# Narrowing float64 weights with a shift, a sign pass and an integer add, in a scan-and-feed-forward kernel on one core

## Chip, cores and metric

The kernel runs on one core of one Trainium2 chip. The metric is the device time in microseconds, the median of several runs. A profile records one execution: every instruction of the engines, every transfer, and the clock that TensorE was granted.

The engines are named as the profile names them: PE is TensorE (PEld its weight loads), DVE is VectorE, ACT is ScalarE, POOL is GpSimd, SP is SyncE, whose queue issues most of the DMAs. Each engine works through its own list of instructions in order and waits on semaphores for the others.

## The reference

Two stages. The first is a chunked state-space scan over 4 batches, 8 heads, 768 positions; the second a feed-forward block of 3072 tokens, 256 to 2048 to 256, with the quick form of GELU.

```python
def _attn_ref(x, a, B, C):
    ...
    for c in range(nc):
        ...
        y_intra = np.einsum('bhij,bhjd->bhid', M, xc)
        y_inter = np.einsum('bhin,bhnd->bhid', Cc, state) * decay_to_i[:, :, :, None]
        y[:, :, sl] = y_intra + y_inter
        ...
        state = decay_full[:, :, None, None] * state + np.sum(Bx, axis=2)
    return y.astype(np.float32)

def _moe_ref(x, w_in, w_out):
    h = x @ w_in
    g = h * (1.0 / (1.0 + np.exp(-1.702 * h)))
    return (g @ w_out).astype(np.float32)
```

The output y of the scan, with its heads side by side, is the x of the feed-forward block. `x`, `a`, `B` and `C` arrive as float32. The two weight matrices `w_in` and `w_out` arrive as float64, and every weight must be made into a float32 on the chip, which has no float64 arithmetic.

## The kernel before

Tokens go in six groups of 512 (g = 0 to 5). For each group the scan gives yT, the transposed input of the feed-forward block. Group 0 then takes the plain way: `hidden(0, f)` (L873) makes the 16 slices of 128 hidden units, each by two fp32 products on PE (each recorded as two passes), followed by a silu on ACT; `project_all(0, ...)` (L975) then multiplies by w_out, for f = 0 to 15, with two products for each f: o[0] for the first 128 output columns (c = 0), o[1] for the second 128 (c = 1). Later groups take a way with fewer products and mixed weights (`first`, `product`, `mix_in`, `mix_w`).

The weights are narrowed while group 0 runs. They come in ten pieces (`PIECES`, L154): 0 to 3 are two hidden slices of w_in each (512 columns), 4 and 5 four slices each (1024 columns), 6 to 9 four slices of w_out each (1024 columns; w_out has the layout partition, c, f, e, so a piece is one stretch of f in each of the two halves c). `fetch` (L163) brings a piece as pairs of 32-bit words. The narrowing takes the words apart: the upper word holds sign, 11 bits of exponent and 20 bits of mantissa, the lower word the rest of the mantissa.

- `fields(i)` (L188): two DVE passes. L192 keeps the exponent bits of the upper word, L195 its mantissa bits with a leading one.
- `clamp(i)` (L198): two ACT passes (L203, L204) that turn the exponent field into a float32 power of two; their bias is a tile, `edge`.
- `rounded(i)` (L206): one DVE pass (L208) that adds the scaled lower word to the mantissa.
- `join(i)` (L215): two DVE passes, L222 puts the sign on the power, L228 multiplies both into w_in or w_out.

Buffers: `bits` four deep, the tiles tagged m and p2 two deep.

The order of every engine is written out by hand: `in_order` (L21) chains the instructions of an engine in the order in which the Python code makes them, so where a call stands decides what it is queued behind. Around the start (L1160 to L1207) the calls are: scores and decays of the first two chunk pairs, `fields(0)`, `ends_first`, `rounded(0)`, `score`, `weigh(0)` (L691), `fetch(1, held=True)` with a memset (L171) that holds back the transfers of pieces 1 to 5, `weigh(1)`, `gain`, `parts_first` (ACT, L730), `clamp(0)`, `keep_first` (DVE, the scan L735 and two copies L740 that give the states S), `finish` (PE: L828 from the decays, L816 from S; then ACT, L845, yT), `join(0)` and so on. Afterwards `at(places, f, ...)` hangs work behind a slice f of `hidden` or ahead of step f of `project_all`: `narrow(i)` (L235, which is `rounded`, the `fields` of the next piece, and `join`) behind slices 1, 2, 4, 6, 9 and 12; for pieces 8 and 9 ahead of projection steps 0, 1 and 5 (L1231 to L1236). Ahead of step 0 also stands `turn(PG)`: four transposes on PE (L597, tp), copies on ACT (L590, BT and CT), then a DVE product (L665, CsT) of the next two chunks.

The framework that builds the program finds for each instruction which earlier instructions wrote or read the same memory, and makes it wait for them by semaphores.

Of the kernel before, what the change touches and what calls it, by code (L numbers as in the profile page):

```python
# [8 lines left out]
FP32 = mybir.dt.float32  # L9
U32 = mybir.dt.uint32  # L10
BF16 = mybir.dt.bfloat16
AF = mybir.ActivationFunctionType
ALU = mybir.AluOpType
AX = mybir.AxisListType

GELU_SCALE = 1.702
P = 128
TG = 512

# [16 lines left out]
def kernel(  # L36
# [31 lines left out]
    nc = tc.nc  # L68
# [7 lines left out]
    DM, DF = moe_w_in.shape[0], moe_w_in.shape[1] // 2  # L76
# [8 lines left out]
    PG = CG // 2  # L85
# [97 lines left out]

    mantissa, power = {}, {}

    def fields(i):  # L188
        hi, cols = bits[i][1], slice(0, PIECES[i][2] * DM)
        mantissa[i] = wide.tile([P, PN], U32, tag="m", name=f"m{i}")[:, cols]  # L190
        power[i] = wide.tile([P, PN], U32, tag="p2", name=f"p2{i}")[:, cols]
        nc.vector.tensor_scalar(out=power[i], in0=hi, scalar1=0x7FF00000, scalar2=None,  # L192
                                op0=ALU.bitwise_and)

        nc.vector.tensor_scalar(out=mantissa[i], in0=hi, scalar1=0x000FFFFF,  # L195
                                scalar2=0x00100000, op0=ALU.bitwise_and, op1=ALU.bitwise_or)

    def clamp(i):  # L198


        e = power[i]
        z = e.bitcast(FP32)
        nc.scalar.activation(z, e, AF.Relu, scale=-8.0, bias=edge[:, 0:1])  # L203
        nc.scalar.activation(e, z, AF.Relu, scale=-1.0, bias=edge[:, 1:2])  # L204

    def rounded(i):  # L206

        nc.vector.scalar_tensor_tensor(out=mantissa[i].bitcast(FP32), in0=bits[i][0],  # L208
                                       scalar=2.0 ** -32, in1=mantissa[i],
                                       op0=ALU.mult, op1=ALU.add)  # L210


    NEXT = {1: (6,), 5: (9,)}
# [1 line left out]
    def join(i, parts=1):  # L215

        name, f, n = PIECES[i]
        n //= parts
        low, m, p2 = bits.pop(i)[1], mantissa.pop(i), power.pop(i)
        for k in range(parts):  # L220
            cols, fs = slice(k * n * DM, (k + 1) * n * DM), slice(f + k * n, f + (k + 1) * n)
            nc.vector.scalar_tensor_tensor(out=p2[:, cols], in0=low[:, cols], scalar=0x80000000,  # L222
                                           in1=p2[:, cols], op0=ALU.bitwise_and, op1=ALU.bitwise_or)
            if name == "in":
                dst, h = w_in[:, fs].rearrange("p f k e -> p (f k e)").unsqueeze(1), 1
            else:
                dst, h = w_out[:, :, fs].rearrange("p c f e -> p c (f e)"), 2
            nc.vector.scalar_tensor_tensor(  # L228
                out=dst, in0=m[:, cols].bitcast(FP32).rearrange("p (h e) -> p h e", h=h),
                scalar=2.0 ** -20, in1=p2[:, cols].bitcast(FP32).rearrange("p (h e) -> p h e", h=h),  # L230
                op0=ALU.mult, op1=ALU.mult)
        for n in NEXT.get(i, ()):
            fetch(n)

    def narrow(i):  # L235
        rounded(i)
        if i + 1 < len(PIECES):
            fields(i + 1)
        join(i, 2 if i == 4 else 1)


# [50 lines left out]
    load(1, "x")  # L292


    edge = const.tile([P, 2], FP32, name="edge")
    nc.vector.memset(edge[:, 0:1], float((896 + 255) << 23))
    nc.vector.memset(edge[:, 1:2], float(255 << 23))
    ones = const.tile([P, P], FP32, name="ones")
    nc.vector.memset(ones, 1.0)

# [276 lines left out]
    def turn(p):  # L577
        turn_only(p)
        since_start(p)
# [106 lines left out]
    def weigh(p, ks=(slice(0, 2),)):  # L686

        Lv = Ls[p].rearrange("p k r q i -> p k r (q i)")
        cb = st[p]["cb"].rearrange("p r k e -> p k r e")
        for k in ks:  # L690
            nc.vector.tensor_tensor(out=Lv[:, k], in0=Lv[:, k], in1=cb[:, k], op=ALU.mult)  # L691
# [172 lines left out]
    gT = {}  # L864
# [8 lines left out]
    def hidden(g, f):  # L873
        j, i = divmod(f, 2)
        if i == 0:
            block(g, j)
        h = bank(f"h{g}_{f}")
        for k in range(NK):
            n = 2 if g == 1 and NK * f + k < 11 else 1
            if n == 2 and NK * f + k < 11 - 8:  # L880
                n = 4
            for e in range(n):
                cols = slice(e * TG // n, (e + 1) * TG // n)
                nc.tensor.matmul(out=h[:, cols], lhsT=w_in[:, f, k], rhs=yT[g][:, k, cols],  # L884
                                 start=(k == 0 and e == 0), stop=(k == NK - 1),
                                 skip_group_check=True)

        nc.scalar.activation(gT[g, j][:, i], h, AF.Silu, scale=GELU_SCALE)


    mixed_in, mixed_y, chain = {}, {}, {}
# [22 lines left out]
        mix(mixed_y[g], yT[g].rearrange("p k (t e) -> p k t e", t=2))  # L914

    def silu(o, i):
        nc.scalar.activation(o, i, AF.Silu, scale=GELU_SCALE)  # L917

    def first(g, j, i):

# [54 lines left out]
    def project_all(g, between):  # L975

        o = [bank(f"o{g}_{c}") for c in range(2)]
        for f in range(NF):
            for do in between.get(f, []):
                do()  # L980
            for c in range(2):
                nc.tensor.matmul(out=o[c], lhsT=w_out[:, c, f],  # L982
                                 rhs=gT[g, f // 2][:, f % 2], start=(f == 0),
                                 stop=(f == NF - 1), skip_group_check=True)
        sums[g] = ffn.tile([P, 2, 2, HT], FP32, tag="gT", name=f"c{g}", bufs=6)
        for c in range(2):
            nc.scalar.activation(sums[g][:, c].rearrange("p t e -> p (t e)"), o[c], AF.Copy,
                                 scale=1.0 / GELU_SCALE)

# [67 lines left out]
    def copies(g):  # L1057
        u = ffn.tile([P, 4, HT], FP32, tag="gT", name=f"u{g}", bufs=6)

        c = ffn.tile([P, 2, 2, HT], FP32, tag="gT", name=f"c{g}", bufs=6)  # L1060

        if g < NG - 1:
            nc.scalar.activation(u[:, 0:4:3], acc[g][1][:, 0:4:3], AF.Copy,
                                 scale=1.0 / GELU_SCALE)
        else:
            nc.scalar.activation(u[:, 0], acc[g][0][0], AF.Copy, scale=1.0 / GELU_SCALE)
            nc.scalar.activation(u[:, 3], acc[g][0][3], AF.Copy, scale=1.0 / GELU_SCALE)
            c = c.rearrange("p t k (c e) -> p c t k e", c=2)
        return u, c

# [2 lines left out]

    def scaled(o, v, w):

        nc.vector.scalar_tensor_tensor(out=o, in0=v, scalar=1.0 / GELU_SCALE, in1=w,
                                       op0=ALU.mult, op1=ALU.add)

    def by_k(t):
# [95 lines left out]
        decay_exp(1, r, ab[1, r])  # L1175
    mask_first(1)
    turn_back()
    fields(0)
    ends_first(0)
    ends_first(1)  # L1180
    rounded(0)
    score(range(PG), since_first)
    weigh(0)
    fetch(1, held=True)
# [1 line left out]
        fetch(i)  # L1186
    rows_a(az, (nc.sync,))
    weigh(1)
    drops()
    gain(range(PG))  # L1190
    parts_first()
    for p in range(PG):
        since_start(p, nc.gpsimd)
    clamp(0)
    keep_first()
    dense(2)
    finish(range(PG))
# [12 lines left out]
    def at(places, i, *work):  # L1210
        places.setdefault(i, []).extend(work)
# [24 lines left out]
    at(in_project[0], 5, lambda: narrow(9))  # L1236
# [203 lines left out]
```

## Time and profile before

| what | value |
|---|---|
| median of 3 runs | 350.04 us (349.7 to 350.7) |
| span of the profiled execution | 348.2 us |
| first matmul, last matmul ends | 1.21 us, 345.40 us |
| DVE passes of the narrowing, 512 columns (L192, L195, L208, L222, L228) | 0.43, 0.42, 0.68, 0.69, 0.69 us |
| the same, 1024 columns | 0.69, 0.69, 1.21, 1.22, 1.23 us |
| ACT passes of the narrowing (L203, L204), 512 and 1024 columns | 0.72 and 1.15 us each |
| hidden products of group 0 (L884) | 17.48 to 47.5 us |
| projection of group 0 (L982) | 47.84 to 81 us |

The profiled execution's span is 1.8 us shorter than the median of the runs: the time outside the program's first and last instruction counts in the one and not in the other. A row of the order of time reads: start and length in us, engine, line and operation, out<-in, shape and count, and in brackets idle time before it with what ended it.

### The profile page before, as it was taken

To read this page: it belongs to the slowest core of one execution; us is meant where nothing else is said; L and a number is where in the kernel's file an instruction comes from. 1 tells how busy PE (TensorE), PEld (TensorE's weight loads), DVE (VectorE), ACT (ScalarE), POOL (GpSimd) and SP (SyncE) were. 2 spreads that over 40 slices of the span, in tenths; PEclk is the share of its full clock that TensorE was granted. 3 is DMA by queue.
4 is the path that set the end of the run, shared out by engine and by line. 5 is a ranking of instruction groups with operands and counts; after the bars stand their busy time and mean duration, and the time that the engine had idled before them with its cause. 6 is when DMAs were issued, how large, how long until landed. Compare 5 with 4: busy or idle time off the path is not lost.

```text
span 348.2 us, 8126 instructions
## 1 busy us (share of the span) xinstructions
PE 341.8 (98%) x3386; PEld 273.1 (78%) x3386; DVE 254.8 (73%) x476; ACT 151.4 (43%) x348; POOL 14.0 (4%) x42
## 2 busy tenths in 40 slices
PE   7899999999999999999999999999999999999996
PEld 6634444557888888888888888888888888899996
DVE  5999999998679998839996548788454654455463
ACT  5598583107354323744342544432554321554320
POOL 8400000100000100000000000000000000000000
PEclk9999999999999999999999999999999999999999
DMA  6599997444527100445703027300000300000301
GB/s 158 118 347 200 260 219 172 78 85 80 107 53 133 44 0 10 69 93 102 111 22 55 2 75 121 65 0 3 0 4 2 61 2 0 0 2 0 62 0 61
DMA packets 89980, 25.92 MB, mean 74 GB/s; under 512 B 73432, under 2 KB 87128, under 8 KB 89944
## 3 DMA queue, kind: packets, MB, share of 16 engines
q1 hardware_dynamic: 89112, 24.88, 34.1%
q10 hardware_dynamic: 832, 0.52, 0.5%
q8 instruction: 26, 0.43, 0.5%
q14 instruction: 10, 0.08, 0.1%
HBM read 22.15 MB, written 3.24 MB: 73 GB/s over the span
## 4 chain that ended last, share of the span: by engine, by line
PE 93%; DMA 3%; DVE 3%; issue 1%; SPq 0%; DVEq 0%
PE acc L1045 28%; PE X L940 19%; PE Y L950 14%; PE h L884 9%; PE o L982 8%; PE acc L1052 7%; PE y L828 2%; PE cb L680 2%; PE y L816 1%; DMA bits<-in_moe_w_in_dram 1%; PE A L711 1%; DMA zB<-in_B_dram 1%; DMA az<-in_a_dram 1%; DVE p L192 1%; DVE m L208 0%
## 5 line engine op out<-in xcount | busy, mean ns | idle before, releaser
L945 ACT ACTIVATE ac<-X 128x256 f32<-128x256 f32 x76 | 29.0, 382 | 78.6 <-PE X L940 78.2
L1045 PE MATMUL acc<-mg,mw 128*128 128x256 f32 x192 | 54.5, 379 | 0.0
L917 ACT ACTIVATE gT<-gT 128x512 f32<-128x512 f32 (+1 forms) x76 | 39.3, 520 | 34.2 <-DVE gT L1072 33.5
L1072 DVE TENSOR_TENSOR gT<-Y,ac 128x512 f32<-128x512 f32 x38 | 26.2, 688 | 36.5 <-PE Y L950 29.9
L940 PE MATMUL X<-my,mi 128*128 128x256 f32 x152 | 45.2, 380 | 0.0
L1072 DVE TENSOR_TENSOR gT<-Y,b 128x256 f32<-128x256 f32 x38 | 15.8, 419 | 34.5 <-PE Y L950 34.5
L1045 PEld LDWEIGHTS acc<-mg,mw 128*128 128x128 f32 x192 | 36.5, 190 | 5.0
L884 PE MATMUL h<-yT,w_in 128*128 128x512 f32 (+2 forms) x108 | 35.7, 486 | 0.6 <-DVE w_in L228 0.6
L1045 PE MATMUL acc<-gT,w_out 128*128 128x256 f32 x128 | 35.5, 379 | 0.0
L884 PEld LDWEIGHTS h<-yT,w_in 128*128 128x128 f32 x108 | 18.3, 190 | 16.4 <-issue 13.2
L940 PEld LDWEIGHTS X<-my,mi 128*128 128x128 f32 x152 | 28.0, 190 | 4.1 <-ACT ac L945 0.4
L982 PE MATMUL o<-gT,w_out 128*128 128x512 f32 x64 | 28.6, 597 | 0.0
L908 DVE TENSOR_TENSOR mg<-gT 128x512 f32<-128x512 f32 x40 | 27.2, 681 | 0.0
L1045 PEld LDWEIGHTS acc<-gT,w_out 128*128 128x128 f32 x128 | 24.2, 190 | 3.4 <-ACT yT L855 0.2
L945 ACT ACTIVATE b<-X 128x256 f32<-128x256 f32 x38 | 14.6, 383 | 20.0 <-PE X L940 19.6
L940 PE MATMUL X<-yT,w_in 128*128 128x256 f32 x76 | 23.2, 389 | 0.0
L950 PE MATMUL Y<-yT,w_in 128*128 128x256 f32 x76 | 22.7, 381 | 0.0
L950 PE MATMUL Y<-my,mi 128*128 128x256 f32 x76 | 22.6, 379 | 0.0
L940 PE MATMUL X<-my,w_in 128*128 128x256 f32 x76 | 22.6, 381 | 0.0
L950 PE MATMUL Y<-yT,mi 128*128 128x256 f32 x76 | 22.5, 379 | 0.0
L982 PEld LDWEIGHTS o<-gT,w_out 128*128 128x128 f32 x64 | 11.8, 190 | 13.2 <-issue 12.4
L402 DVE TENSOR_TENSOR_SCAN L<-a,idents 128x1024 f32<-128x1024 f32 x9 | 20.5, 2278 | 0.4 <-DMA a<-scratch 0.4
(154 smaller groups left out, 544.5 us busy)
## 6 DMA issues: line engine op xcount, KB each, us to landing
a<-scratch SPq DMA_DIRECT2D x18, 256.0 KB, 5.2
bits<-in_moe_w_out_dram SPq DMA_DIRECT2D x8, 512.0 KB, 5.7
x<-in_x_dram SPq DMA_DIRECT2D x24, 128.0 KB, 3.3
out_dram<-ob SPq DMA_DIRECT2D x40, 64.0 KB, 1.9
bits<-in_moe_w_in_dram SPq DMA_DIRECT2D x8, 256.0 KB, 4.5
bits<-in_moe_w_in_dram SPq DMA_DIRECT2D x4, 512.0 KB, 9.2
b<-in_B_dram SPq DMA_DIRECT2D x20, 64.0 KB, 3.0
af<-in_a_dram SPq DMA_DIRECT2D x3, 384.0 KB
```

Of the source, the lines that this page charges most:

```text
L402: nc.vector.tensor_tensor_scan(out=L, data0=ra[p].rearrange("p k e -> p (k e)"), data1=idents.rearrange("p h i -> p (h i)"), initial=0.0, ...
L680: nc.tensor.matmul(out=s["cb"][side, r, k].rearrange("p (q i) -> p q i", q=Q), lhsT=BT[rows, k, side], rhs=CT[rows, k, :, side], start=Tru ...
L884: nc.tensor.matmul(out=h[:, cols], lhsT=w_in[:, f, k], rhs=yT[g][:, k, cols], start=(k == 0 and e == 0), stop=(k == NK - 1), skip_group_ch ...
L908: nc.vector.tensor_tensor(out=t[:, 0:2], in0=B[:, :, 1], in1=B[:, 0], op=ALU.subtract)
L917: nc.scalar.activation(o, i, AF.Silu, scale=GELU_SCALE)
L940: nc.tensor.matmul(out=s["X"], lhsT=lhsT, rhs=rhs, start=i == "1", stop=i == "4", skip_group_check=True)
L945: nc.scalar.activation(copy, s["X"], AF.Copy)
L950: nc.tensor.matmul(out=o, lhsT=lhsT, rhs=rhs, start=s.pop("new", False), stop=i != "5", skip_group_check=True)
L982: nc.tensor.matmul(out=o[c], lhsT=w_out[:, c, f], rhs=gT[g, f // 2][:, f % 2], start=(f == 0), stop=(f == NF - 1), skip_group_check=True)
L1045: nc.tensor.matmul(out=acc[g][0][i][:, cols], lhsT=w, rhs=h[:, cols], start=(j == 0 and k == 0 and (i, 0) in begins), stop=(j == NF // 2 - ...
L1052: nc.tensor.matmul(out=o[k] if type(o) is list else o[:, cols], lhsT=h[:, cols], rhs=w, start=(j == 0 and (i, k) in begins), stop=(j == NF ...
L1072: nc.vector.tensor_tensor(out=o, in0=v, in1=w, op=ALU.add)
```

## The change

A weight is now narrowed in another way. ACT makes two tiles of a piece (`unpack`): the upper word read as a float32 and scaled by 2 to the power -112, and the lower word scaled by 2 to the power -29 with 2 to the power 23 added. DVE then shifts the first left by three bits and clears its top bit (`shift`), puts the sign bit of the upper word on the second (`sign`), and adds both as unsigned 32-bit integers into w_in or w_out (`join`). The weight that results is twice the right one, and the constants of the silu and of the final scale carry the factor (WEIGHT). The tile `edge` is no longer needed.

The calls are placed anew: `unpack(0)` where `fields(0)` stood, `shift(0)` and `sign(0)` behind `weigh(1)`, `unpack(i + 1)` where `clamp(i + 1)` stood, and `narrow(i)` is now shift, sign and join of the same piece.

```diff
+WEIGHT = 2.0
...
-    def fields(i):
-        hi, cols = bits[i][1], slice(0, PIECES[i][2] * DM)
...
-        nc.vector.tensor_scalar(out=power[i], in0=hi, scalar1=0x7FF00000, scalar2=None,
-                                op0=ALU.bitwise_and)
-        nc.vector.tensor_scalar(out=mantissa[i], in0=hi, scalar1=0x000FFFFF,
-                                scalar2=0x00100000, op0=ALU.bitwise_and, op1=ALU.bitwise_or)
-    def clamp(i):
...
-        nc.scalar.activation(z, e, AF.Relu, scale=-8.0, bias=edge[:, 0:1])
-        nc.scalar.activation(e, z, AF.Relu, scale=-1.0, bias=edge[:, 1:2])
-    def rounded(i):
-        nc.vector.scalar_tensor_tensor(out=mantissa[i].bitcast(FP32), in0=bits[i][0],
-                                       scalar=2.0 ** -32, in1=mantissa[i],
-                                       op0=ALU.mult, op1=ALU.add)
+    high, low = {}, {}
+
+    def unpack(i):
+        cols = slice(0, PIECES[i][2] * DM)
+        high[i] = wide.tile([P, PN], U32, tag="m", name=f"m{i}")[:, cols]
+        low[i] = wide.tile([P, PN], U32, tag="p2", name=f"p2{i}")[:, cols]
+        words_low, words_high = bits[i]
+        nc.scalar.activation(high[i].bitcast(FP32), words_high.bitcast(FP32), AF.Copy,
+                             scale=2.0 ** -112)
+        nc.scalar.activation(low[i], words_low, AF.Copy, scale=2.0 ** -29, bias=2.0 ** 23)
+
+    def shift(i):
+        nc.vector.tensor_scalar(out=high[i], in0=high[i], scalar1=3, scalar2=0x7FFFFFFF,
+                                op0=ALU.logical_shift_left, op1=ALU.bitwise_and)
+
+    def sign(i):
+        nc.vector.scalar_tensor_tensor(out=low[i], in0=bits.pop(i)[1], scalar=0x80000000,
+                                       in1=low[i], op0=ALU.bitwise_and, op1=ALU.bitwise_or)
...
     def join(i, parts=1):
...
-            nc.vector.scalar_tensor_tensor(out=p2[:, cols], in0=low[:, cols], scalar=0x80000000,
-                                           in1=p2[:, cols], op0=ALU.bitwise_and, op1=ALU.bitwise_or)
             if name == "in":
                 dst, h = w_in[:, fs].rearrange("p f k e -> p (f k e)").unsqueeze(1), 1
             else:
                 dst, h = w_out[:, :, fs].rearrange("p c f e -> p c (f e)"), 2
-            nc.vector.scalar_tensor_tensor(
-                out=dst, in0=m[:, cols].bitcast(FP32).rearrange("p (h e) -> p h e", h=h),
-                scalar=2.0 ** -20, in1=p2[:, cols].bitcast(FP32).rearrange("p (h e) -> p h e", h=h),
-                op0=ALU.mult, op1=ALU.mult)
+            nc.vector.tensor_tensor(
+                out=dst.bitcast(U32), in0=y[:, cols].rearrange("p (h e) -> p h e", h=h),
+                in1=q[:, cols].rearrange("p (h e) -> p h e", h=h), op=ALU.add)
...
     def narrow(i):
-        rounded(i)
-        if i + 1 < len(PIECES):
-            fields(i + 1)
+        shift(i)
+        sign(i)
         join(i, 2 if i == 4 else 1)
...
-        nc.scalar.activation(gT[g, j][:, i], h, AF.Silu, scale=GELU_SCALE)
+        nc.scalar.activation(gT[g, j][:, i], h, AF.Silu, scale=GELU_SCALE / WEIGHT)
...
-    fields(0)
+    unpack(0)
     ends_first(0)
     ends_first(1)
-    rounded(0)
     score(range(PG), since_first)
     weigh(0)
     fetch(1, held=True)
...
     weigh(1)
+    shift(0)
+    sign(0)
     drops()
     gain(range(PG))
     parts_first()
...
-    clamp(0)
     keep_first()
...
     join(0)
-    fields(1)
-    clamp(1)
+    unpack(1)
     table(AF.Silu)
-    rounded(1)
-    fields(2)
-    clamp(2)
-    join(1)
+    unpack(2)
+    narrow(1)
     load(PG)
...
         at(in_hidden[0], k, lambda i=i: narrow(i))
-        at(in_hidden[0], c, lambda i=i: clamp(i + 1))
+        at(in_hidden[0], c, lambda i=i: unpack(i + 1))
...
-    at(in_project[0], 0, lambda: turn(PG), lambda: rounded(8), lambda: fold_ident(1),
-       lambda: fields(9), lambda: join(8))
-    at(in_project[0], 1, lambda: clamp(9))
+    at(in_project[0], 0, lambda: turn(PG), lambda: shift(8), lambda: sign(8),
+       lambda: fold_ident(1), lambda: join(8))
+    at(in_project[0], 1, lambda: unpack(9))
```

More of the change, by code (lines that the diff above doesn't have):

```diff
@@ L182, in fetch @@
         bits[i] = t[:, :, 0], t[:, :, 1]
-    mantissa, power = {}, {}
-    def fields(i):
-        hi, cols = bits[i][1], slice(0, PIECES[i][2] * DM)
-        mantissa[i] = wide.tile([P, PN], U32, tag="m", name=f"m{i}")[:, cols]
-        power[i] = wide.tile([P, PN], U32, tag="p2", name=f"p2{i}")[:, cols]
-        nc.vector.tensor_scalar(out=power[i], in0=hi, scalar1=0x7FF00000, scalar2=None,
-                                op0=ALU.bitwise_and)
-        nc.vector.tensor_scalar(out=mantissa[i], in0=hi, scalar1=0x000FFFFF,
-                                scalar2=0x00100000, op0=ALU.bitwise_and, op1=ALU.bitwise_or)
-    def clamp(i):
-        e = power[i]
-        z = e.bitcast(FP32)
-        nc.scalar.activation(z, e, AF.Relu, scale=-8.0, bias=edge[:, 0:1])
-        nc.scalar.activation(e, z, AF.Relu, scale=-1.0, bias=edge[:, 1:2])
-    def rounded(i):
-        nc.vector.scalar_tensor_tensor(out=mantissa[i].bitcast(FP32), in0=bits[i][0],
-                                       scalar=2.0 ** -32, in1=mantissa[i],
-                                       op0=ALU.mult, op1=ALU.add)
+    high, low = {}, {}
[13 more added lines that the diff above has]
+                                       in1=low[i], op0=ALU.bitwise_and, op1=ALU.bitwise_or)
     NEXT = {1: (6,), 5: (9,)}
@@ L218, in join @@
         n //= parts
-        low, m, p2 = bits.pop(i)[1], mantissa.pop(i), power.pop(i)
+        y, q = high.pop(i), low.pop(i)
         for k in range(parts):
             cols, fs = slice(k * n * DM, (k + 1) * n * DM), slice(f + k * n, f + (k + 1) * n)
-            nc.vector.scalar_tensor_tensor(out=p2[:, cols], in0=low[:, cols], scalar=0x80000000,
-                                           in1=p2[:, cols], op0=ALU.bitwise_and, op1=ALU.bitwise_or)
             if name == "in":
@@ L292 @@
     load(1, "x")
-    edge = const.tile([P, 2], FP32, name="edge")
-    nc.vector.memset(edge[:, 0:1], float((896 + 255) << 23))
-    nc.vector.memset(edge[:, 1:2], float(255 << 23))
     ones = const.tile([P, P], FP32, name="ones")
@@ L916, in silu @@
     def silu(o, i):
-        nc.scalar.activation(o, i, AF.Silu, scale=GELU_SCALE)
+        nc.scalar.activation(o, i, AF.Silu, scale=GELU_SCALE / WEIGHT)
     def first(g, j, i):
@@ L987, in project_all @@
             nc.scalar.activation(sums[g][:, c].rearrange("p t e -> p (t e)"), o[c], AF.Copy,
-                                 scale=1.0 / GELU_SCALE)
+                                 scale=1.0 / (GELU_SCALE * WEIGHT))
     mixed_w, mixed_g, acc = {}, {}, {}
@@ L1063, in copies @@
             nc.scalar.activation(u[:, 0:4:3], acc[g][1][:, 0:4:3], AF.Copy,
-                                 scale=1.0 / GELU_SCALE)
+                                 scale=1.0 / (GELU_SCALE * WEIGHT))
         else:
-            nc.scalar.activation(u[:, 0], acc[g][0][0], AF.Copy, scale=1.0 / GELU_SCALE)
-            nc.scalar.activation(u[:, 3], acc[g][0][3], AF.Copy, scale=1.0 / GELU_SCALE)
+            nc.scalar.activation(u[:, 0], acc[g][0][0], AF.Copy, scale=1.0 / (GELU_SCALE * WEIGHT))
+            nc.scalar.activation(u[:, 3], acc[g][0][3], AF.Copy, scale=1.0 / (GELU_SCALE * WEIGHT))
             c = c.rearrange("p t k (c e) -> p c t k e", c=2)
@@ L1074, in scaled @@
     def scaled(o, v, w):
-        nc.vector.scalar_tensor_tensor(out=o, in0=v, scalar=1.0 / GELU_SCALE, in1=w,
+        nc.vector.scalar_tensor_tensor(out=o, in0=v, scalar=1.0 / (GELU_SCALE * WEIGHT), in1=w,
                                        op0=ALU.mult, op1=ALU.add)
```

## Prediction

> **What bounds the kernel now.** I read the page's head first, then the waits of TensorE, then the order of time on TensorE, then on VectorE and ScalarE around the places where the narrowing of the weights meets it.
>
> ```profile
> span 348.2 us, 8126 instructions
> PE 341.8 (98%) x3386; PEld 273.1 (78%) x3386; DVE 254.8 (73%) x476; ACT 151.4 (43%) x348; POOL 14.0 (4%) x42
> ...
> PE h L884 <- DVE w_in L228: 0.6, 1, 0.6
> ```
>
> TensorE is busy 98% of the span, and in the list of what its matmuls waited for only one row names the narrowing. The span is 348.2 us, the median of the runs 350.04: 1.8 us lie around the span, and I add them at the end.
>
> ```profile
> 11.74 2.35 DVE L691 TENSOR_TENSOR L<-L,cb 128x1024 f32<-128x1024 f32 x2
> 14.02 1.22 DVE L735 TENSOR_TENSOR_SCAN steps<-drop,steps 128x512 f32<-128x512 f32 x1
> ...
> 15.81 1.67 PE L816 MATMUL y<-CsT,S 32*64 32x64 f32 x56
> 17.48 3.70 PE L884 MATMUL h<-yT,w_in 128*128 128x512 f32 x8
> 21.74 13.97 PE L884 MATMUL h<-yT,w_in 128*128 128x512 f32 x32 [0.57 <-DVE w_in L228]
> ...
> 47.84 3.60 PE L982 MATMUL o<-gT,w_out 128*128 128x512 f32 x8
> ```
>
> (Order of time: start, length, engine, line, what.) Two places matter. In the head, the scan at L735 gives S, S gives y (L816), y gives yT and the first hidden product at 17.48; at 21.18 TensorE waits 0.57 for piece 1. From there on it never waits for a weight: the projection (L982) starts at 47.84, each fp32 product being two records of about 0.43 (3.60 for eight).
>
> **The change part by part.** *Passes removed.* A piece of 1024 columns has now five VectorE passes, 0.69 + 0.69 + 1.21 + 1.22 + 1.23 = 5.0 us (L192, L195, L208, L222, L228), and would have three: shift like L192, sign like L222, add like L228, 3.1 us. For a piece of 512: 2.9 to 1.8. Four small and six large pieces save 4 x 1.1 + 6 x 1.9 = 15.8 us of VectorE. ScalarE's twenty passes lose their bias operand: the nearest row without one, L888 at 0.59 for 512, stands against 0.72 at L203; some 2.4 us in all. TensorE hides all of this but the 0.57 above, so that is the most it can bring.
>
> *Head.* L691 starts at 11.74 because the second score (L680) ends at 11.62; the passes taken from ahead of it ended at 11.82 and are worth 0.08 at most. But shift(0) and sign(0) now stand between the second L691 and the scan. Their price is the spacing of such starts: 0.34 (L192 at 18.07 to L195 at 18.41) and 0.60 (L208 at 11.14 to L691 at 11.74), 0.94 together. GpSimd's L665 runs to 14.13 beside shift(0); the first L192 took 1.72 instead of 0.43 beside GpSimd's L648, so up to 0.3 more; below, 0 if the scan keeps its place. I take 0.94: scan, S, y, yT and the first hidden product slip to 18.42. The ScalarE passes of piece 0 fill an idle 1.17 us before L517 and cost nothing; past that they would push L517 by 0.1. Piece 1 is due at 18.42 + 3.70 = 22.12. Its way: yT's copies end at 18.08 + 0.94 = 19.02, two ScalarE passes of 0.6 to 20.2, sign 0.7 to 20.9, add 0.7 to 21.6. In time: the wait of 0.57 goes. The head nets +0.37 (bounds -0.57 and +0.7). The weights' DMAs leave at the same time, behind the memset that follows the first L691.
>
> *Projection: a new wait.* The built program's list of waits shows what the diff doesn't:
>
> ```
> 210 L972 Matmult o_0_669<-gT_0_498,w_out 128x512 [waits DVE_49,Activation_49]
> 211 L972 Matmult o_1_670<-gT_0_498,w_out 128x512 [waits DVE_49,Activation_49]
> ...
> 225 L972 Matmult o_1_670<-gT_2_530,w_out 128x512 [waits DVE_49]
> ```
>
> Before, row 211 waited for ScalarE alone, and VectorE was waited for at f = 0, 4, 8 and 12, where each piece of w_out is first used. Counting VectorE's signals up to the awaited value, row 211 (f = 0, second half of the columns) now waits for the add of piece 8, and row 225 (f = 5) for that of piece 9. The add writes both column halves through one bitcast view; the waits are those of a view taken as one stretch of memory from its first to its last word, which for piece 8 covers the second half's f = 0 to 11. So the projection can't pass f = 0 before piece 8, needed only at f = 8, is narrowed. When is that?
>
> ```profile
> 47.61 0.60 ACT L888 ACTIVATE gT<-h 128x512 f32<-128x512 f32 x1 [0.86 <-PE h L884]
> ...
> 50.68 0.83 ACT L590 ACTIVATE CT<-tp,part 128x256 f32<-128x256 f32 x2
> ...
> 51.55 0.42 DVE L665 TENSOR_TENSOR CsT<-tp,since 128x256 f32<-128x256 f32 x1 [0.41 <-PE tp L597]
> 51.89 1.22 DVE L208 SCALAR_TENSOR_TENSOR m<-bits,m 128x1024 f32<-128x1024 uint32 x1
> ...
> 56.36 1.23 DVE L228 SCALAR_TENSOR_TENSOR w_out<-m,p 128x1024 f32<-128x1024 f32 x1
> ```
>
> ScalarE's order there is unchanged: last silu, two passes of piece 8, BT, CT; then VectorE's L665. The silu slips 0.37 with the head, the two passes (L203 and L204 now, 1.15 each) shrink from 2.3 to about 2.1, so L665 starts again at about 51.55. From there by starts: L665 to shift 0.34, shift to sign 0.60, sign to idents 1.13 (L208 at 51.89 to L335 at 53.02), idents to add 0.60, add 1.23: it ends at 55.45. After L228 ended at 21.60 TensorE started at 21.74, so 0.14 more: 55.6. TensorE has done its one allowed product at 47.84 + 0.37 + 0.86 = 49.07. It stands still for 6.5 us, and everything behind it in its order (all of the projection, tp, scores, the later groups) is late by that.
>
> Piece 9: row 225 waits for its add, which in turn waits for the f = 4 product of the second half (the same kind of overlap). TensorE fills the add's 1.23 + 0.14 us with one product of 0.86: 0.5 us more. The VectorE work between (L402 to L665, 57.50 to 63.63 now) starts 1.8 us earlier, at the landing of a at 55.7, and isn't late.
>
> *The clock.* A standstill of 6.5 us is longer than any in this trace.
>
> ```profile
> core 0: us, PE busy (x) PEld busy (x) DVE busy (x) ACT busy (x) POOL busy (x), PEclk, DMA share, GB/s
> 345.40:348.80 3.40, 0.00 (x1) 0.00 (x0) 0.29 (x1) 0.00 (x0) 0.00 (x0) 1.00 0.35 116
> 348.90:350.00 1.10, 0.00 (x0) 0.00 (x0) 0.00 (x0) 0.00 (x0) 0.00 (x0) 0.50 0.00 0
> ...
> 1.21 2.93 PE L440 MATMUL busy<-ones 128*128 128x192 f32 x8 [1.21 <-DVE ones L299]
> ```
>
> Behind the last matmul (345.40) the granted clock (PEclk) is whole for 3.4 us and half from about 348.9. At the start eight 192-column records take 2.93, 0.37 each, where 0.43 x 192 / 512 = 0.16 would do: half speed for about the first 2.9 us. So the clock should fall in the standstill and halve the next 2.9 us: 1.45 us lost. Bounds: 0, and twice 1.45 if the recovery needs two such stretches. I take 1.45, the start's own row.
> The Trainium skill (TensorE: Matmul & The Clock Gate, Part 1) says that the clock is judged in free-running windows of about 3.4 us and falls only after a whole idle one; by that a standstill of 6.5 us would nearly always, not always, hold one, and the half-speed stretch would cost about 1.7, for 0.25 us more in all.
>
> *The add itself.* It is no ordinary add: the listing has it as an instruction of its own kind, on 2048 half words for 1024 words. No two-input row on half words is in the trace. Bounds: 1.21 (as many cycles as words, like L691) and 2.28 (the scan at L402, two cycles for each of 1024). I take 1.23, being the same bytes as L228; at 2.28 both stalls grow by 1.05.
> The Trainium skill (VectorE: DVE Perf Modes, Mode 2×_1P) allows two packed 16-bit elements in a cycle for two inputs of step 1, which fits the low bound; if this instruction has no such mode the sum rises by 2.1, an estimate from that page.
>
> Sum: 348.2 + 0.37 + 6.5 + 0.5 + 1.45 = 357.0 of span; with 1.8 around it 358.8 us.
>
> **The rivals.** (1) The same stall, but the clock stays up: 357.4. For it: the fall comes only some 3.5 us into an idle stretch, and the trace has no fall within the work. (2) The add at one half word a cycle: 358.8 + 2.1 = 360.9. For it: every two-input row of the trace runs at one element a cycle; against it: half words can be packed. (3) The other side: the projection is not held up, because what row 211 awaits is done by 49.1, so that only the head counts: 350.04 + 0.37 = 350.4, and 349.5 if the scan keeps its place too. It would decide if the awaited add were that of piece 7, done before 51.14 now and some microseconds sooner with fewer passes; against it stands the count of signals, and that piece 8 can't be ready before CT is copied. (4) Fewer passes don't get VectorE out of anyone's way: true wherever TensorE doesn't wait, and already in the sum.
>
> **How the numbers follow.** Forecast 0.60, (1) 0.18, (2) 0.15, (3) 0.07. Time 358.8. The range goes from (1) with the head's lower bound, 357.4 - 0.9 = 356.5, to (2) with the head's and a little of the clock's upper bound, 361.5. A measurement of this kernel tells about 0.3%, 1.05 us, from no change: (3) lies mostly within it, so faster 0.02, same 0.05, slower 0.93.
>
> **What would show it.** In the new profile: TensorE idle for some 6 us after the first product of the projection, put down to VectorE's add; a second, short one before f = 5; PEclk below 9 in the slice after; the first hidden product near 18.4 and no wait for piece 1; adds of about 0.7 and 1.23. It is wrong if L982's successor runs through from f = 0, or if the adds of pieces 8 and 9 stand elsewhere in VectorE's order.

## The result, and the profile after

The changed kernel takes 362.13 us (median of 4 runs, 360.6 to 365.24) against 349.95 for the kernel before beside it (349.7 to 350.7): ratio 1.0333, 95% interval 1.0275 to 1.0391. It is slower by 12.2 us; the prediction said 8.8, and its range ended at 361.5. The profiled run is the slowest of the four, 365.24 us, with a span of 363.3 against 348.2. Medians are of all runs, ratios of those within 1.5% of the fastest of their kernel, which leaves out one of twelve in experiment 1 and three of twelve in the first version of experiment 6, all four with a lowered clock.

The page of the changed kernel first: span, TensorE's busy time, and the clock that TensorE was granted in 40 slices of the span.

```profile
span 363.3 us, 8119 instructions
...
PE 346.9 (95%) x3386; PEld 274.5 (76%) x3386; DVE 239.9 (66%) x453; ACT 150.3 (41%) x348; POOL 14.2 (4%) x42
...
PEclk9999987789999999999999999999999999999999
```

VectorE has 14.9 us less to do (15.8 predicted), ScalarE 1.1 less (2.4 predicted), and TensorE stands still as it never did before. What its matmuls waited for (us in total, times, longest):

```profile
PE o L972 <- DVE w_out L223: 10.1, 2, 6.4
...
PE A L701 <- DMA x<-in_x_dram: 0.8, 1, 0.8
```

Both waits are the projection's, for adds into w_out. In order of time (start, length, engine, line, operation; in brackets the idle time before it and what ended it):

```profile
48.13 1.02 PE L972 MATMUL o<-gT,w_out 128*128 128x512 f32 x2
...
54.22 1.22 DVE L223 CUSTOM_DVE_ANT_0 w_out<-m,p 128x2048 uint16<-128x2048 uint16 x1
...
55.59 4.37 PE L972 MATMUL o<-gT,w_out 128*128 128x512 f32 x6 [6.44 <-DVE w_out L223]
...
60.59 2.29 DVE L392 TENSOR_TENSOR_SCAN L<-a,idents 128x1024 f32<-128x1024 f32 x1 [5.15 <-DMA a<-scratch]
...
68.79 1.23 DVE L223 CUSTOM_DVE_ANT_0 w_out<-m,p 128x2048 uint16<-128x2048 uint16 x1
...
70.07 6.11 PE L972 MATMUL o<-gT,w_out 128*128 128x512 f32 x7 [3.66 <-DVE w_out L223]
```

The first standstill is the predicted one: one product at 48.13, then 6.44 us until piece 8's add is done. The second, at f = 5 for piece 9's add, was predicted at 0.5 and is 3.66. The scan L392, which stands ahead of piece 9's passes in VectorE's queue, waited 5.15 us for the DMA of a, landed at 60.5; before it landed at 55.7.

The clock, in stretches of about 3.41 us (columns as in the prediction's fence; the last three are granted clock, DMA share, GB/s):

```profile
48.50:51.90 3.40, 0.65 (x2) 0.00 (x0) 0.82 (x3) 3.02 (x5) 0.00 (x0) 1.00 1.01 160
51.92:55.32 3.40, 0.00 (x0) 0.00 (x0) 3.40 (x5) 0.00 (x0) 0.00 (x0) 0.50 1.11 307
55.34:58.73 3.39, 3.14 (x4) 1.51 (x5) 0.10 (x1) 0.72 (x1) 0.00 (x0) 0.50 1.04 199
58.75:62.15 3.40, 3.40 (x12) 1.72 (x11) 1.55 (x1) 2.52 (x5) 0.00 (x0) 1.00 0.70 165
65.58:68.97 3.39, 0.83 (x2) 0.00 (x1) 3.12 (x5) 0.00 (x0) 0.74 (x1) 1.00 0.93 125
68.99:72.38 3.39, 2.31 (x3) 1.18 (x4) 1.02 (x1) 0.00 (x0) 0.00 (x0) 0.50 0.23 66
72.40:75.80 3.40, 3.40 (x5) 1.35 (x4) 0.00 (x0) 0.00 (x0) 0.00 (x0) 0.50 0.76 94
```

The clock halves twice, behind stretches with 0.65 and 0.83 us of work in them, and comes back only behind a full or nearly full one (3.40 and 3.14). Work at half clock loses half its time: (58.74 - 55.59) / 2 = 1.58, and (75.81 - 70.07) / 2 = 2.87.

These terms make up the whole difference, in this profile and in a second one of the changed kernel (told below), set against a second one of the kernel before:

| term, us | predicted | this profile | second profile |
|---|---|---|---|
| start of the projection | +0.37 | 48.13 - 47.84 = 0.29 | 49.85 - 47.27 = 2.58 |
| first wait (f = 0) | 6.5 | 6.44 | 6.42 |
| half clock behind it | 1.45 | 1.58 | 2.83 |
| second wait (f = 5) | 0.5 | 3.66 | 0.46 |
| half clock behind it | 0 | 2.87 | 0 |
| sum | 8.8 | 14.84 | 12.29 |
| difference of the spans | | 363.3 - 348.2 = 15.1 | 360.1 - 347.5 = 12.6 |

The two profiles lose their time in different places. The second has no second standstill to speak of and no clock fall behind it; 1.7 of its 2.58 at the start of the projection is a fall of the clock in the head (half speed from 18.60 to 22.01), and the half clock behind the first standstill takes nearly twice as long. Of the other three runs beside the result only the time and the mean clock are known: 0.99 in one, which is 6.83 us at half clock, and 0.981 in two, 13.65 us. The second figure fits two standstills, as in the first profile, and also one standstill and the head, so it doesn't tell them apart.

So three things were open: whether the waits are due to the adds' view, why a is late, and what the clock costs.

### The profile page after: what moved, and what is told of

Same layout as the page of the kernel before. It is cut to its first block, busy times and chain, and to the rows that moved or that the text cites. A ratio compares the mean times of both kernels' runs of the same rounds, so it can differ in the third digit from the quotient of the medians.

```text
span 363.3 us, 8119 instructions
## 1 busy us (share of the span) xinstructions
PE 346.9 (95%) x3386; PEld 274.5 (76%) x3386; DVE 239.9 (66%) x453; ACT 150.3 (41%) x348; POOL 14.2 (4%) x42
## 4 chain that ended last, share of the span: by engine, by line
PE 79%; DMA 7%; DVE 6%; SPq 4%; issue 2%; ACTq 1%; ACT 0%; POOL 0%; DVEq 0%; POOLq 0%
PE acc L1035 24%; PE X L930 17%; PE Y L940 12%; PE acc L1042 7%; PE o L972 6%; PE h L874 5%; DMA a<-scratch 4%; SPq L181 2%; DMA az<-in_a_dram 2%; PE cb L670 2%; PE y L818 2%; PE y L806 1%; SPq L265 1%; DVE L L392 1%; PE A L701 1%
## 5 line engine op out<-in xcount | busy, mean ns | idle before, releaser
L972 PE MATMUL o<-gT,w_out 128*128 128x512 f32 x64 | 33.5, 675 | 10.1 <-DVE w_out L223 10.1
L972 PEld LDWEIGHTS o<-gT,w_out 128*128 128x128 f32 x64 | 13.3, 218 | 26.6 <-issue 21.9
L874 PEld LDWEIGHTS h<-yT,w_in 128*128 128x128 f32 x108 | 18.3, 190 | 16.1 <-issue 12.6
L392 DVE TENSOR_TENSOR_SCAN L<-a,idents 128x1024 f32<-128x1024 f32 x9 | 20.5, 2279 | 5.8 <-DMA a<-scratch 5.8
## 6 DMA issues: line engine op xcount, KB each, us to landing
bits<-in_moe_w_in_dram SPq DMA_DIRECT2D x4, 512.0 KB, 12.6
```

The costliest lines, as they stand in the source:

```text
L392: nc.vector.tensor_tensor_scan(out=L, data0=ra[p].rearrange("p k e -> p (k e)"), data1=idents.rearrange("p h i -> p (h i)"), initial=0.0, ...
L972: nc.tensor.matmul(out=o[c], lhsT=w_out[:, c, f], rhs=gT[g, f // 2][:, f % 2], start=(f == 0), stop=(f == NF - 1), skip_group_check=True)
```

## Experiments

The kernel before ran beside each group at 350.92 to 351.62 (single runs 349.58 to 354.0), 1 to 1.7 us above its 349.95 beside the result. Ratios below are to the runs beside the experiment; expectations in plain microseconds were written against 350 and read some 1 to 1.6 us low.

**1. No overlap at all.** Each add into w_out is made in two, one per half of the columns, so that each writes one unbroken stretch.

```diff
-            nc.vector.tensor_tensor(
-                out=dst.bitcast(U32), in0=y[:, cols].rearrange("p (h e) -> p h e", h=h),
-                in1=q[:, cols].rearrange("p (h e) -> p h e", h=h), op=ALU.add)
+            a, b = (v[:, cols].rearrange("p (h e) -> p h e", h=h) for v in (y, q))
+            if i in SPLIT:
+                for c in range(h):
+                    nc.vector.tensor_tensor(out=dst[:, c].bitcast(U32), in0=a[:, c],
+                                            in1=b[:, c], op=ALU.add)
+            else:
+                nc.vector.tensor_tensor(out=dst.bitcast(U32), in0=a, in1=b, op=ALU.add)
```

with `SPLIT = (6, 7, 8, 9)`.

> Each add into w_out is made as two, one for each half of the columns, so that none covers a stretch that is not its own; the rest is the changed kernel. Theory A (the two standstills come from the add's view being taken as one stretch of memory): the projection runs through from f = 0, no fall of the clock, and only the head's +0.3 is left: 350.3 us (349.8 to 350.8), the longest wait of the projection's matmuls under 0.3. Theory B (the standstills come from the new passes themselves being late, or from the integer add as an instruction of its own kind): the waits stay, 360 to 365.

Measured 352.02 (350.03 to 355.8), ratio 1.0029 [0.9999, 1.0059]: 0.8 us above the kernel before beside it, where 0.3 was expected. The projection waits for no add. All of the slowdown beyond the head goes with the views: theory A. The integer add itself, still an instruction of its own kind, brings no wait (theory B falls). The multiply before wrote the same two runs of each piece in one instruction and made no such wait either; whether the view on half words or the kind of instruction is what the framework takes as one stretch was not separated. In the head, something the first profile didn't show: `y` waits 1.4 us for S, and 8 of the 12 runs have a mean clock of 0.99 to 0.995.

```profile
17.35 1.68 PE L811 MATMUL y<-CsT,S 32*64 32x64 f32 x56 [1.39 <-DVE S L735]
```

**2. One view at a time.** `SPLIT = (8,)`, then `SPLIT = (9,)`.

> Only the add of piece 8 is made in two; that of piece 9 stays one. Theory A with the two standstills hiding one another: the projection passes f = 0 at once and is at f = 5 at 48.13 + 11 products of 0.86 + 4 transposes, about 58.1. It waits there for the add of piece 9, which stands 9.5 us behind the scan that waits for the DMA of a: 65.2 if a lands at 55.7 as in the kernel before, 70.0 if at 60.5 as in the changed kernel. Wait 7.1 to 11.9, and one fall of the clock for 1.5 to 3: 359 to 365 us, hardly better than the changed kernel. Theory C (the second standstill is only an after-effect of the first, by late copies or a slow clock): 350.3 to 351.5.

Measured 363.32 (362.19 to 364.65), ratio 1.0342 [1.0304, 1.038]: no better than the changed kernel, as expected. The one wait (7.1 to 11.9 expected), and VectorE's queue behind it:

```profile
PE o L977 <- DVE w_out L230: 12.1, 1, 12.1
```

```profile
60.98 2.29 DVE L397 TENSOR_TENSOR_SCAN L<-a,idents 128x1024 f32<-128x1024 f32 x1 [5.04 <-DMA a<-scratch]
...
65.00 1.76 DVE L488 TENSOR_TENSOR_SCAN since<-af,first 128x768 f32<-128x768 f32 x1 [0.54 <-POOL af L481]
...
69.36 1.23 DVE L230 CUSTOM_DVE_ANT_0 w_out<-m,p 128x2048 uint16<-128x2048 uint16 x1
```

From the landing of a (60.86) to the end of the add (70.59) are 9.7 us of work in a fixed order, with no wait for TensorE in it. The second standstill is no after-effect of the first (theory C falls); the first hides most of it. Undoing one wait of two gains nothing.

> Only the add of piece 9 is made in two; that of piece 8 stays one. The first standstill stays (6.4) with its slow stretch (1.6), the second goes with its slow stretch, since the add of piece 9 is due only at f = 12: 350.3 + 8.0 = 358.3 us (357.8 to 358.9), mean clock 0.990. If the second standstill had another cause than the view, it stays: 361 to 365.

Measured 361.61 (359.87 to 363.82), ratio 1.0296 [1.0254, 1.0337]: 10.4 us over before, where 8.0 were expected. The second wait is gone, the first is 6.4. The missing microseconds are clock in this profile: the half clock behind the standstill lasts to 63.41, (63.41 - 57.34) / 2 = 3.0 instead of 1.6, and one more stretch of half clock lies in the head (19.04 to 22.45).

**3. The clock alone.** The same kernel with seven products of no use in the standstill.

```diff
+                if f == 0 and c == 1:
+                    spare = area("spare")
+                    for _ in range(7):
+                        nc.tensor.matmul(out=spare[:, 0], lhsT=ones, rhs=gT[g, 0][:, 0],
+                                         start=True, stop=True, skip_group_check=True)
```

> As with only the add of piece 9 in two, and 7 products of ones and a hidden tile, 6.0 us, go to a spare bank in the first standstill; their result is not used. If the fall of the clock is due to TensorE's idleness and costs 1.6: no fall, the matmuls behind the standstill at 0.43, 350.3 + 6.4 = 356.7 us (356.2 to 357.2). If the fall costs nothing or comes from something else: no difference to the version without them, 358.3.

Measured 359.34 (358.11 to 360.88), ratio 1.0232 [1.0191, 1.0274]. TensorE in the former standstill:

```profile
49.09 6.17 PE L980 MATMUL spare<-gT,ones 128*128 128x512 f32 x14
55.77 2.81 PE L982 MATMUL o<-gT,w_out 128*128 128x512 f32 x6 [0.51 <-DVE w_out L230]
```

Six records take 2.81 here, 0.47 each, and 4.37 in the changed kernel. The mean clock is whole in three of the four runs. Work that computes nothing makes the kernel 2.3 us faster (361.61 - 359.34; the two intervals just overlap, the mean clocks, 0.976 to 0.99 and 0.995 to 1.0, don't). So TensorE's idleness causes the fall, and its price is about that; part of the 2.3 may be the slow stretch in the head, which the filler doesn't touch and which only the profile without it has. The expected 356.7 was missed by 2.6; 1.2 of that is the higher level of the runs beside it, and the profile has a single pause of 1.8 us, ahead of a `y` product at 267 us, that nothing in the trace explains.

**4. Piece 9's place in the queue.** What stood ahead of it is put behind it.

```diff
-    at(in_project[0], 2, lambda: decay(PG + 1), lambda: clip_rows(1),
-       lambda: decay_rows(1), lambda: turn(PG + 1))
     at(in_project[0], 5, lambda: narrow(9))
+    at(in_project[0], 5, lambda: decay(PG + 1), lambda: clip_rows(1),
+       lambda: decay_rows(1), lambda: turn(PG + 1))
```

> The changed kernel, with the work of the projection's slot 2 (the scan that waits for a, the row decays, the copies of the second pair) put behind the narrowing of piece 9 at f = 5; both adds stay one. Theory F (the second standstill comes from the place of piece 9's add in VectorE's queue, behind a scan that waits for a DMA): it shrinks to the 0.5 of the prediction, and no second fall of the clock: before + 0.3 + 6.4 + 0.5 + 1.6 to 3.0 = before + 8.8 to 10.2. Theory G (it comes from late bits of piece 9, or from the add's own wait for the product of f = 4): before + 11 to 15, as the changed kernel.

Measured 359.79 (359.43 to 359.92), ratio 1.0251 [1.0216, 1.0286]: before + 8.9, theory F. That this is nearly the predicted 8.8 is luck: there is no second wait at all here, and the half clock takes 2.5 instead of 1.45 ((60.75 - 55.75) / 2). VectorE and then TensorE around f = 5:

```profile
58.59 1.23 DVE L206 SCALAR_TENSOR_TENSOR p<-bits,p 128x1024 uint32<-128x1024 uint32 x1 [0.34 <-ACT p L197]
66.23 1.23 DVE L223 CUSTOM_DVE_ANT_0 w_out<-m,p 128x2048 uint16<-128x2048 uint16 x1 [6.42 <-PE o L972]
```

```profile
55.75 10.45 PE L972 MATMUL o<-gT,w_out 128*128 128x512 f32 x18 [6.40 <-DVE w_out L223]
...
66.47 7.32 PE L972 MATMUL o<-gT,w_out 128*128 128x512 f32 x16
```

The passes of piece 9 end at 59.8 and its add waits 6.42 us for the product of f = 4, not the other way round; the transposes that now stand at f = 5 cover what was left of the wait.

**5. Why a is late.** Both kernels once more.

> The kernel before once more, for the landing of its DMAs and the start of its scan in the head on the same chip as the runs beside it. Theory D (the change itself makes the transfers late): the first piece of a for the second half lands near 55.7 again and the scan starts near 14.0. Theory E (they vary from one execution or chip to the next, whatever the kernel): landing anywhere from 55 to 61, as in the changed kernels (58.7 to 61.5), and hardly a cost, since the add of piece 9 is due only at f = 12.

> The changed kernel once more. The first wait of the projection is 6.4 again. The second follows the landing of a: it ends 9.5 us behind it (plus 0.14). With a at 58.7 to 61.5 the add ends at 68.2 to 71.0 and the wait is 2 to 5 us; the mean clock tells whether the second fall of the clock came (0.98) or not (0.99).

Before: 349.17, a at 55.52, scan at 14.07. Changed: 361.79, a at 58.22, second wait 0.46, clock 0.986, the last column of the table above. The wait is under the 2 to 5 us expected because TensorE too came late: it reaches f = 5 at 69.37 instead of 66.41. Two profiles of the kernel before have a at 55.5 and 55.7; all eight of kernels with the change so far at 58.2 to 61.5. That is theory D: not chance. And the first piece of x, whose load is issued before any pass of the narrowing runs (at 5.5 to 5.8; no pass starts before 8.5), lands at 9.1 and 9.2 in the one and at 9.6 to 10.0 in the others. What differs so early isn't work but place. The built programs list these addresses in a partition:

```
            edge    ones    x     bits0   bits9   a
before     50336   50368  64768   79104   87296  79104
changed        -   50336  64736   79072   87264  79072
```

The change drops the tile `edge`: 8 bytes, 32 with its padding. Every buffer behind it moves down by 32, from multiples of 64 to 32 past one. The landing buffers listed (x, bits0, bits9, a) even stood on multiples of 256, so the runs can't tell which of 64, 128 and 256 matters, only what 32 bytes beside them costs. Three runs test that, all with one line in front of `ones`:

```diff
+    const.tile([P, 2], FP32, name="spare")
```

> The changed kernel with one unused tile of 8 bytes (it takes 32) where the tile edge stood. The change takes that tile out, and with it every buffer behind it, the landing buffers of x, b, the weights and a among them, stands 32 bytes lower: at 32 past a multiple of 64 bytes, where it stood on a multiple of 64. Theory H (transfers into such buffers are slower, and that is why a lands 3 to 6 us later than before): a lands at 55.5 to 56 again, the first piece of x at 9.1, the add of piece 9 is ready when TensorE comes to f = 5, the second wait is about 0.5 and no second fall of the clock: the 358.8 us of the prediction, 358.0 to 359.6. Theory I (the transfers are late because ScalarE now reads the landing buffers, or by chance): no change to the changed kernel, a at 58 to 61.5 and 360 to 365.

> All adds into w_out in two, the head's passes moved as in the run on the head, and the unused tile. By theory H the transfers are those of the kernel before, the scan starts at 14.0, the first hidden product at 17.5, no wait of TensorE for a late copy in the second half: span 347.4 to 348.0, before - 0.3 (-0.8 to +0.3). By theory I: as the run on the head, before + 0.3, with a at 59 to 60 and single runs up to 355.

> The kernel before with the same unused tile more, which moves every buffer behind it by 32 bytes, off the multiples of 64; nothing else. By theory H: the first piece of x lands at 9.6 to 10.0, the second piece of weights 5 at 29.4 to 31.2, a at 58 to 61.5; the head starts its scan 0.5 to 1 later and the end moves by that: before + 0.5 to 1.5, single runs up to 355. By theory I: no difference to the kernel before, a at 55.5 to 55.7.

The third moves the kernel before off the multiples of 64 and changes nothing else. The four microseconds in which pieces 4 and 5 load, the 16 engines full in each, one line per kernel: before, before with the shift, changed, changed with the tile.

```profile
22.00:26.00 4.00, 4.00 (x10) 1.72 (x10) 3.94 (x8) 3.93 (x8) 0.00 (x0) 1.00 1.09 386
```

```profile
22.00:26.00 4.00, 3.37 (x8) 1.63 (x9) 3.90 (x8) 3.92 (x8) 0.00 (x0) 1.00 1.08 361
```

```profile
22.00:26.00 4.00, 4.00 (x11) 1.75 (x10) 3.12 (x6) 3.20 (x6) 0.00 (x0) 1.00 1.09 359
```

```profile
22.00:26.00 4.00, 4.00 (x11) 1.72 (x10) 2.86 (x5) 3.52 (x8) 0.00 (x0) 1.00 1.10 381
```

386 and 381 GB/s on multiples of 64, 361 and 359 off them, whichever way the weights are narrowed. Over all fourteen profiles of this study:

| buffers | profiles | GB/s, 22 to 26 us | first x lands | a lands |
|---|---|---|---|---|
| on multiples of 64 | 5 | 381 to 388 | 9.05 to 9.37 | 55.1 to 56.7 |
| 32 past one | 9 | 350 to 361 | 9.64 to 10.01 | 58.2 to 61.5 |

Theory H is shown for the transfers. SP's queue hands the delay on, since some of its loads wait for an earlier one to land: with the shift alone the kernel before issues this load of a at 51.37 instead of 48.70, and it lands at 58.90 instead of 55.66. Where between 58.2 and 61.5 it lands in one execution stays unexplained. In time: the shift alone makes the kernel before 1.0032 [1.0005, 1.0059] (352.82), with a lowered clock in 2 of its 12 runs; its scan starts at 14.38, less late than expected. The changed kernel with the tile measured 361.81, ratio 1.0296 [1.0267, 1.0325]; its second wait is the predicted one, 0.46:

```profile
56.91 5.46 PE L973 MATMUL o<-gT,w_out 128*128 128x512 f32 x6 [6.44 <-DVE w_out L223]
...
69.40 5.85 PE L973 MATMUL o<-gT,w_out 128*128 128x512 f32 x13 [0.46 <-DVE w_out L223]
```

but it is before + 10.3, not + 8.8, and so within the times that theory I gave: the half clock behind the first standstill takes 2.8 here ((62.49 - 56.91) / 2), and the head has one more stretch of it (18.12 to 21.53).

**6. The head.** shift(0) goes ahead of the first L<-L,cb product, sign(0) behind the copies of S, all adds in two.

```diff
     score(range(PG), since_first)
+    shift(0)
     weigh(0)
...
-    shift(0)
-    sign(0)
     drops()
...
     keep_first()
+    sign(0)
     dense(2)
```

> All adds into w_out in two, and in the head shift(0) ahead of the first L<-L,cb product and sign(0) behind the copies of S. The scan keeps the place it had before the change, so that S, y and the first hidden product lose the 0.94 that the two passes cost in the version with all adds in two; the wait of 0.57 for piece 1 stays away. Before - 0.6 (-0.9 to 0), that is 0.9 less than the version with all adds in two. If the head's slip was not the two passes: no difference to that version, before + 0.3 to 0.8.

Measured 351.27 (348.98 to 355.55), ratio 1.0006 [0.9974, 1.0038]; the scan starts at 14.42 instead of 15.57, 4 of 12 runs show a lowered clock instead of 8. That is 0.35 above the kernel before, not 0.6 under it as expected; the profile still waits 0.4 us for piece 1. With the tile as well (expectation under 5): 349.25 (348.87 to 350.55, 7 runs), ratio 0.9941 [0.9919, 0.9962], the only version whose interval lies under 1; no run with a lowered clock. The gain of 2.3 us is more than the 0.3 (at most 0.8) expected. The last run completes the square:

> All adds into w_out in two and the unused tile, so that the landing buffers stand on multiples of 64 bytes, but the head's two passes where the change put them. It completes the square of head and buffers: neither mended 1.0029 of before, head alone 1.0006, both 0.9941. If the head's passes cost what the prediction took for them (0.94 at the start of the first hidden product, net 0.4 or less, and in some executions a fall of the clock for 1.7 more): before - 1 to 0 in most executions, up to before + 1 in some, ratio 0.997 to 1.001. If the buffers were all of it: 0.994.

Measured 351.63 (349.81 to 353.66), ratio 0.9999 [0.9974, 1.0025].

| all adds in two | buffers 32 off | on multiples of 64 |
|---|---|---|
| head as the change has it | 1.0029 | 0.9999 |
| head's passes moved | 1.0006 | 0.9941 |

With the buffers in place the two passes cost 0.0058 of the time, about 2 us, not the 0.4 net of the prediction (the two intervals are apart); with the buffers 32 off the difference, 0.0023, is within the intervals. VectorE, then TensorE, in the last run, which has the tile but not the moved passes:

```profile
13.83 0.65 DVE L201 TENSOR_SCALAR m<-m 128x512 uint32<-128x512 uint32 x1
14.40 0.67 DVE L206 SCALAR_TENSOR_TENSOR p<-bits,p 128x512 uint32<-128x512 uint32 x1
14.99 1.21 DVE L731 TENSOR_TENSOR_SCAN steps<-drop,steps 128x512 f32<-128x512 f32 x1
```

```profile
15.38 0.48 PE L824 MATMUL y<-L,x 64*32 64x64 f32 x33 [0.56 <-issue]
16.78 1.68 PE L812 MATMUL y<-CsT,S 32*64 32x64 f32 x56 [0.92 <-DVE S L736]
```

and its clock in the two stretches behind:

```profile
15.35:18.74 3.39, 2.44 (x90) 2.17 (x91) 2.14 (x4) 1.01 (x4) 0.00 (x0) 1.00 0.90 257
18.76:22.15 3.39, 3.39 (x5) 1.35 (x4) 1.81 (x3) 3.36 (x8) 0.00 (x0) 0.50 0.88 247
```

The wait of 0.92 lies in a stretch of small products, and at its end, at 18.75, the clock falls; the first hidden products run 3.41 us at half speed, 1.7 lost. Neither the wait nor the work alone decides: in experiment 1's profile the wait of 1.39 brought no fall, though the stretch that holds most of it (13.56 to 16.97) has only 2.09 us of work. The mean clock is lowered in 6 of this kernel's 12 runs, and in 1 of the 69 runs of the kernel before beside the experiments.

## Why the prediction was wrong

**Right.** The waits read from the built program: f = 0 for piece 8 after one product, f = 5 for piece 9, nothing else. The first standstill, 6.5, measured 6.40 to 6.44 in five profiles. The adds at about 0.7 and 1.23, the same bytes at the same rate as the multiply, so rival (2) fell, though its 360.9 came nearest the median: luck, for its reason was wrong. ScalarE's two passes of piece 8 at 2.13 for 2.1 predicted. Rival (1) fell with the clock rows, rival (3) with the waits, and experiment 1 shows what it would have been.

**The step that failed** stands under piece 9: "The VectorE work between (L402 to L665, 57.50 to 63.63 now) starts 1.8 us earlier, at the landing of a at 55.7, and isn't late." I let VectorE start when the DMA landed, and took the landing from the trace of before as if the change couldn't touch it. In the result's profile it landed at 60.5, the add of piece 9 ended at 70.0 instead of some 65, and TensorE, at f = 5 at 66.41, waited 3.66 instead of 0.5 and lost another 2.87 to the clock: together 6.0 us of the 6.3 by which this profile's difference exceeds the sum. The landing moved because the diff removes `edge`, a line to which the prediction gave no price: what it moved was every address behind it. "The weights' DMAs leave at the same time" held within half a us (12.55 and 13.01 in the two profiles of the changed kernel, 13.01 and 12.93 in those of the kernel before), but they arrive later: the last of the pieces held back lands at 31.17 and 29.43 instead of 28.23 and 28.52.

This step doesn't carry every run. In the second profile of the changed kernel a lands late too, the second wait is 0.46 as predicted, and the kernel is still outside the range at 361.79: there the term that failed is the clock, mis-sized behind the first standstill (2.83 instead of 1.45) and put at nothing in the head. How the two share in the median is open.

**Sizes.** The clock was taken as one slow stretch of 2.9 us, costing 1.45. The slow time behind the first standstill is what is left of the stretch in which work resumes, plus a full one if that stretch isn't full enough (3.14 us of work was enough, 2.65 in experiment 2's second version wasn't): 1.58 to 3.0 lost. A second standstill of 3.66 added 2.87, where the prediction saw none because it took that wait for 0.5. The head's net of 0.37 was 0.29 in the result's profile and 2.58 in the second; where it can be counted, in the versions without a standstill, 8 and 6 of 12 runs lose some 1.7 more to a fall of the clock, which the prediction didn't look for. And the 0.57 for piece 1, named as the most that the change could bring, isn't in the second profile of the kernel before at all.

The Trainium skill (TensorE: Matmul & The Clock Gate, Part 1) has windows of about 3.4 us, a fall after at least one idle window and a rise after a busy one. The lengths agree: every slow stretch within the work is 3.41, 6.83, 10.24 or 13.65 us. The fall agrees at three of the standstills, where it came only behind a stretch without any work. At four others it came behind a stretch with 0.65 to 1.15 us of recorded work, and in the head behind stretches with 1.83 to 2.44, which aren't idle.

Not settled: why transfers into buffers 32 bytes off a multiple of 64 are slower, since the runs show only that they are; and why single runs of the kernel before spread from 349.6 to 352.9 at whole clock, which leaves open what the 2.3 us of the one faster version are. Its profiled span, 347.4, is no shorter than that of the second profile of the kernel before, 347.5.

## What to carry to other kernels

A diff changes addresses as well as instructions: look at where the buffers land before taking a DMA's arrival from the old trace. Once a new wait ties two engines together, every slack of the old trace is to be read again, and a wait hidden behind another shows only when the first is mended: take them away together. Price a standstill of a few microseconds with the clock it costs, not as idle time alone.

## What the runs showed of the hardware

That 32 bytes in a landing buffer's address show in its loads at all. The Trainium skill (SBUF — State Buffer, Operand start alignment) says that transfers at any element-aligned address are correct and that its runs timed nothing; here, where all addresses are element-aligned, buffers 32 bytes beside a multiple of 256 loaded at 350 to 361 GB/s and buffers on one at 381 to 388, some 7% apart.

That TensorE's clock can fall after a wait of 0.92 us with only small products around it, and needn't after one of 1.39. And that an unsigned 32-bit add, which VectorE runs as an instruction of its own on 16-bit halves, takes 0.69 us for 512 and 1.22 for 1024 words, no more than the float multiply it replaces.
